# Two-layer feed-forward after retention: shifted loads in the first layer only, four groups, two banks begun with partial sums, another order of conversions, second pass backwards

## The chip, the core and the metric

The kernel runs on one core of one Trainium2 chip. The metric is the time of one execution on the device in microseconds (us). The number to predict is a median of runs of the changed kernel.

TensorE is called PE here (PEld are its weight loads), VectorE is DVE, ScalarE is ACT, GpSimd is POOL, and SP is the engine whose queue issues every DMA of this kernel.

## The reference

```python
# retention: B=2, H=8, S=768, D=64
for t in range(S):
    state = gamma * state + k[t] outer v[t]
    y[t] = scale * q[t] @ state
x = y as (1536 tokens, 512)
h = x @ moe_w_in                      # 512 -> 2048
x = softplus(h) @ moe_w_out           # 2048 -> 512   (layer 1)
h = x @ moe2_w_in
out = silu(h) @ moe2_w_out            #               (layer 2)
```

The four weight matrices are 64-bit floats in memory.

## The kernel before

Every matrix product is made of three matmuls: a float is kept as a high part (rounded to the fast format fp32r) and a low part (the rest), and low·high, high·low and high·high are added up in PSUM.

**Conversion of weights.** A weight tile of 128 x 512 64-bit numbers (512 KB) is brought in by `w_load` into one of three buffers (`rc`, "raw"). ACT takes the exponent (`w_exponent`, L357). DVE takes the digits (`w_digits`) and forms the low part (`w_values`, L378 to L386). ACT forms the high part (`w_split`, L399). For tiles from number `NEAR` on, a second load of the same tile, displaced by two bytes (`near_load`, L339), lets one shift (L364) give the digits, which otherwise takes two operations (L369, L370).

**Layer 1** runs in 48 steps. The 16 blocks of 128 inner columns (`fc`) are cut into groups (`GROUPS`), and within a group the three token blocks of 512 follow one another. A step does `first(i)` (12 matmuls into bank `h`, L447, then softplus on ACT) and `second(i - 2)` (12 matmuls into four banks `acc0` to `acc3`, L486). At the end of a group and block, `evacuate` adds the four banks to `part` on DVE (L497; the first group copies instead). PE's order is thus first, second, first, second. Conversions of later tiles are laid into the steps by `_jobs`, which goes through the steps, gains `STEP_ROOM` in each and spends `TILE_COST` or `FORMS_COST`. A job has three parts: a start (exponent), a main part in the same step, and an end in the next step.

**Layer 2** uses a seven-product scheme (products P1 to P7 of quarter matrices). Its weights need, beside conversion, sums of quarters: `w_sums` and `w_keep`, together called "forms". The two `w_in` tiles of a pair (s = 0) are converted into the buffer `st1`; forms turns `st1` into seven quarters with low parts, and one DMA stores them to DRAM (`d1`, L420, 1792 KB). The `w_out` tiles (s = 1) are converted into `st2` and stored to `d2` (L403, 512 KB). `w32` is scratch for the sums. Later `q1_load` (L563) and `q2_load` (L567) bring the stored forms back. There are 8 pairs of blocks and 2 passes over the tokens, so 16 pair steps, q0 to q15. What layer 1's steps had no room for is left for the first pair steps, in "slots" after some of the products: a slot ends the job before, and does the main part of the next one.

In a pair step, products P1, P6, P2, P7, P5, P4, P3 (L580) alternate with "fill": the second matmuls (L612) of the pair before. Between products ACT and DVE work on the banks: ACT copies P1's bank into P6's (L652), and keeps the others (L655, L661); DVE makes c22 after P5 (L664) and c12 after P3 (L670); ACT does silu twice (L594, L595) and DVE the low part (L596). P3 adds into the bank that L664 has read, so it waits for L664. Every engine and SP's queue work strictly in program order.

## Time and profile before

| | |
|---|---|
| median of 3 runs | 607.4 us (606.79 to 607.94) |
| the profiled execution: its own time | 611.62 us |
| the profiled execution: span of its instructions | 609.2 us |
| PE busy, of the span | 567.9 us (93%) |
| DVE busy | 366.1 us (60%) |
| ACT busy | 245.2 us (40%) |
| mean granted TensorE clock | 0.974 of full speed |

The busy shares are means over stages of different kinds: retention (to about 66 us), layer 1 (to about 306 us), layer 2 with conversions still running (to about 440 us), and layer 2 alone. All times inside the program below are us from the start of the span.

### The profile page before, as it was taken

How to read it: one execution, taken by the hardware profiler on the slowest of the kernel's cores; microseconds unless marked ns; L12 is line 12 of the kernel's file. 1: busy time of each engine (PE TensorE's matmuls, PEld its weight loads, DVE VectorE, ACT ScalarE, POOL GpSimd, SP SyncE). 2: the span in 40 equal slices, each digit the busy share in tenths (PEclk: the TensorE clock that was granted, in tenths of full speed). 3: DMA queues.
4: the chain of work that ended last, by engine and by line, in shares of the span. 5: the costliest groups of instructions: out<-in, count | busy, mean ns of one | idle time of the engine just before them, and what ended most of it. 6: DMA issues, size and time to landing. Idle time of an engine off the chain costs nothing.

```text
span 609.2 us, 8166 instructions
## 1 busy us (share of the span) xinstructions
PE 567.9 (93%) x3122; PEld 485.7 (80%) x3122; DVE 366.1 (60%) x642; ACT 245.2 (40%) x461; POOL 25.6 (4%) x24
## 2 busy tenths in 40 slices
PE   7899999999999999999997689496899999999997
PEld 5777888888888888888886578386788999999996
DVE  3877847987888789768846757566464222122212
ACT  2354535544344433435443535244354433333332
POOL 1554000000000000000000000000000000000000
PEclk9999999999999999999998989697899999999999
DMA  8993323886848777777459999898374754445412
GB/s 304 357 386 115 105 103 105 305 280 210 294 152 297 248 247 292 275 267 280 167 202 357 384 333 411 299 409 323 153 280 180 277 207 190 190 189 190 190 69 103
DMA packets 32453, 148.10 MB, mean 243 GB/s; under 512 B 3616, under 2 KB 3616, under 8 KB 28064
## 3 DMA queue, kind: packets, MB, share of 16 engines
q1 hardware_dynamic: 32416, 147.60, 66.1%
q8 instruction: 24, 0.39, 0.3%
q14 instruction: 13, 0.11, 0.0%
HBM read 121.37 MB, written 26.21 MB: 242 GB/s over the span
## 4 chain that ended last, share of the span: by engine, by line
PE 75%; DMA 12%; DVE 8%; ACT 2%; issue 2%; SPq 0%; DVEq 0%; ACTq 0%
PE acc L486 21%; PE h L447 21%; PE acc L612 15%; DMA d<-st 7%; PE by L580 6%; PE bz L580 4%; PE bx L580 4%; DMA rr<-in_att 3%; DMA rc<-in_wts 1%; PE sc L231 1%; DMA rp<-in_att 1%; PE py L249 1%; DVE w L407 1%; DVE rc L381 1%; PE py L271 1%
## 5 line engine op out<-in xcount | busy, mean ns | idle before, releaser
L447 PE MATMUL h<-rx,rw 128*128 128x512 f32 (+1 forms) x588 | 139.4, 386 | 0.1
L486 PE MATMUL acc<-rg,rw 128*128 128x512 f32 x564 | 136.5, 390 | 0.0
L612 PE MATMUL acc<-rw,rg 128*128 128x512 f32 x477 | 130.6, 405 | 0.0
L447 PEld LDWEIGHTS h<-rx,rw 128*128 128x128 f32 x588 | 108.6, 188 | 22.4 <-DVE rx L294 0.3
L486 PEld LDWEIGHTS acc<-rg,rw 128*128 128x128 f32 x564 | 105.7, 188 | 21.8 <-issue 0.4
L612 PEld LDWEIGHTS acc<-rw,rg 128*128 128x128 f32 x477 | 92.2, 196 | 12.9
L466 ACT ACTIVATE rg<-h 128x512 fp32r<-128x512 f32 x47 | 28.0, 597 | 115.5 <-PE h L447 115.5
L596 DVE TENSOR_TENSOR rg<-re,rg 128x384 fp32r<-128x384 f32 x53 | 29.3, 557 | 72.3 <-ACT re L595 72.3
L386 DVE SCALAR_TENSOR_TENSOR st<-rc 128x512 fp32r<-128x512 int32 x32 | 22.2, 692 | 44.5 <-DMA d<-st 43.7
L381 DVE SCALAR_TENSOR_TENSOR rc<-rc 128x512 uint32<-128x512 uint32 x64 | 44.3, 692 | 2.2
L357 ACT ACTIVATE rc<-rc 128x512 f32<-128x512 f32 x64 | 41.8, 668 | 5.4 <-DMA rc<-in_wts 3.9
L399 ACT ACTIVATE st<-rc 128x512 fp32r<-128x512 f32 x32 | 20.0, 632 | 49.3 <-DMA d<-st 43.2
L580 PE MATMUL bz<-f,rw 128*128 128x384 f32 x96 | 22.3, 373 | 17.9 <-DVE rp L664 17.9
L378 DVE TENSOR_SCALAR rc<-rc 128x512 uint32<-128x512 uint32 x64 | 27.0, 422 | 19.5 <-ACT rc L357 19.5
L594 ACT ACTIVATE rg<-rp 128x384 fp32r<-128x384 f32 x32 | 16.7, 522 | 49.0 <-DVE rp L670 24.8
L580 PEld LDWEIGHTS bz<-f,rw 128*128 128x128 f32 x96 | 18.8, 208 | 20.6 <-DVE rp L664 19.6
L473 DVE TENSOR_TENSOR rg<-re,rg 128x512 fp32r<-128x512 f32 x47 | 34.0, 723 | 1.1 <-ACT re L467 1.0
L497 DVE TENSOR_TENSOR rp<-acc,rp 128x512 f32<-128x512 f32 x48 | 31.0, 684 | 4.2 <-PE acc L486 4.2
L580 PE MATMUL by<-rx,rw 128*128 128x384 f32 x144 | 29.8, 342 | 2.9 <-ACT rp L655 2.9
L580 PEld LDWEIGHTS by<-rx,rw 128*128 128x128 f32 x144 | 26.4, 193 | 5.8 <-ACT rp L655 3.4
L580 PE MATMUL by<-f,rw 128*128 128x384 f32 x144 | 29.3, 338 | 0.0
L384 DVE TENSOR_SCALAR rc<-rc 128x512 uint32<-128x512 uint32 x64 | 27.3, 427 | 2.2
(82 smaller groups left out, 630.1 us busy)
## 6 DMA issues: line engine op xcount, KB each, us to landing
rc<-in_wts SPq DMA_DIRECT2D x64, 512.0 KB, 5.0
rw<-d SPq DMA_DIRECT2D x16, 1792.0 KB, 7.9
near<-in_wts SPq DMA_DIRECT2D x53, 511.5 KB, 4.6
rw<-d SPq DMA_DIRECT2D x16, 1024.0 KB, 9.7
d<-st SPq DMA_DIRECT2D x8, 1792.0 KB, 7.0
d<-st SPq DMA_DIRECT2D x16, 512.0 KB, 5.4
rp<-in_att SPq DMA_DIRECT2D x8, 512.0 KB, 7.0
out<-rp SPq DMA_DIRECT2D x12, 256.0 KB, 2.0
```

The source lines that it names most:

```text
L357: nc.scalar.activation(out=z, in_=raw_t[u][:, :, 1].bitcast(F32), func=AF.Copy, scale=2.0**-112)
L378: nc.vector.tensor_scalar(out=z, in0=z, scalar1=3, scalar2=4, op0=ALU.logical_shift_left, op1=ALU.bitwise_or)
L381: nc.vector.scalar_tensor_tensor(out=a, in0=raw[:, :, 1], scalar=0x80000000, in1=z, op0=ALU.bitwise_and, op1=ALU.bitwise_or)
L384: nc.vector.tensor_scalar(out=z, in0=a, scalar1=0xFF800000, scalar2=None, op0=ALU.bitwise_and)
L447: nc.tensor.matmul(ph[:, t], lhsT=w[:, s], rhs=x[:, kc, t], start=kc == o == j == 0, stop=kc == NPAIR - 1 and j == 2, skip_group_check=i == 0,
L466: nc.scalar.activation(out=ghi, in_=ph, func=AF.Softplus)
L473: nc.vector.tensor_tensor(out=glo, in0=t, in1=ghi.bitcast(F32), op=ALU.subtract)
L486: nc.tensor.matmul(acc_t[m], lhsT=lhsT, rhs=rhs, start=(first and j == 0), stop=(last and j == 2))
L497: nc.vector.tensor_tensor(out=to, in0=acc_t[m], in1=to, op=ALU.add)
L580: nc.tensor.matmul(to, lhsT=a[:, s], rhs=x[:, kc, :], start=start and kc == j == 0, stop=kc == 1 and j == 2, skip_group_check=True,)
L596: nc.vector.tensor_tensor(out=glo, in0=r, in1=ghi.bitcast(F32), op=ALU.subtract)
L612: nc.tensor.matmul(acc2_t[m], lhsT=a[:, s], rhs=b, start=start and j == 0, stop=stop and j == 2)
```

## The change

- `GROUPS` becomes (3, 4, 4, 5): four groups instead of five, so 12 evacuations of four banks instead of 15.
- Banks 0 and 1 (`SEEDED`) are no longer added to `part` by DVE. When a group ends, ACT copies the bank out to `part`, then copies the sum so far of the next group and block into the bank, and that block's matmuls all accumulate on it. Banks 2 and 3 are added by DVE as before.
- Of a layer 2 pair, the order is now: both s = 0 tiles, forms, both s = 1 tiles. The s = 1 tile of an odd block goes to `w32` instead of `st2`. The end of forms is divided: ACT's copy (`w_sums_high`) comes at the start of the next slot, DVE's subtraction and the store (`w_keep`) at its end.
- The displaced loads stop with the last tile of layer 1's steps. The tiles left for layer 2's slots use the two-operation digits.
- `_jobs` has other numbers: 20 tiles and 5 forms of layer 2 are done in layer 1's steps instead of 16 and 3, and 12 tiles and 3 forms are left instead of 16 and 5. A pair step has three slots (P1, P6, P5) instead of four.
- The second pass takes the pairs from 7 to 0, so two of `q1_load` and two of `q2_load` fall away at the turn. `q1_load(0)` is issued after step 45 instead of 41, and the preparation of layer 2's left operands is one step earlier.

```diff
-GROUPS = (3, 3, 3, 3, 4)
+GROUPS = (3, 4, 4, 5)
+SEEDED = (0, 1)
...
-STEP_ROOM = 5.0
+STEP_ROOM = 5.3
...
-        second += [("tile", 1, 2 * p + j, s) for j in range(2) for s in range(2)] + [("forms", 1, p, 0)]
+        a, b = 2 * p, 2 * p + 1
+        second += [("tile", 1, a, 0), ("tile", 1, b, 0), ("forms", 1, p, 0), ("tile", 1, a, 1), ("tile", 1, b, 1)]
...
+        k = (0, 1, 2, 1, 0, 2)[u] if u < 6 else (1, 0, 2)[u % NRAW]
...
     def near_load(u):
-        if u >= len(tiles):
+        if u >= NEAR[1]:
...
-            hi, lo = st2[:, 0:512], st2[:, 512:1024]
+            t = (st2, w32)[fc % 2]
+            hi, lo = t[:, 0:512], t[:, 512:1024]
...
+    def w_sums_high():
         nc.scalar.activation(out=st1[:, 1024:2048].bitcast(F32R), in_=st1[:, 3072:4096], func=AF.Copy)
...
-                    acc_t[m], lhsT=lhsT, rhs=rhs, start=(first and j == 0), stop=(last and j == 2)
+                    start=first and j == 0 and not seeded,
...
-            if g > 0:
+            if m in SEEDED:
+                nc.scalar.activation(out=to, in_=acc_t[m], func=AF.Copy)
+                if i + 1 < N and steps[i + 1][0] > 0:
+                    acc_t[m] = psa.tile([P, BLK], F32, tag=f"acc{m}", name=f"acc{i + 1}_{m}")
+                    b1 = steps[i + 1][1]
+                    nc.scalar.activation(out=acc_t[m], in_=part[:, m, b1 * BLK : (b1 + 1) * BLK], func=AF.Copy)
+            elif g > 0:
                 nc.vector.tensor_tensor(out=to, in0=acc_t[m], in1=to, op=ALU.add)
...
+    def pair_of(q):
+        return q if q < NPR else 2 * NPR - 1 - q
...
-        if q < NQ:
-            nc.sync.dma_start(out=q1[q % 2], in_=d1[q % NPR])
+        if q < NQ and not NPR <= q < NPR + 2:
+            nc.sync.dma_start(out=q1[pair_of(q) % 2], in_=d1[pair_of(q)])
...
+    def job_last(j):
+        if j[0] == "forms":
             w_keep(j[2])
...
-            if i == 41:
+            if i == 45:
                 q1_load(0)
...
-                work = {"P1": (slot,), "P6": (slot,), "P7": (slot,), "P5": (slot,)}
+                work = {"P1": (slot,), "P6": (slot,), "P5": (slot,)}
```

How the rows stand on the engines, at three places. First DVE, in a pair step of layer 2 before: from one forms to the next writing of `st_883` (that is `st1`; `w_884` is `w32`, `st_885` is `st2`).

```order
L413 TENSOR_TENSOR st_883<-w_884,st_883 128x256
L596 TENSOR_TENSOR rg<-re,rg 128x384 x2
L670 TENSOR_TENSOR rp<-bz_2751,rp 128x384
L596 TENSOR_TENSOR rg<-re,rg 128x384
L417 TENSOR_TENSOR st_883<-st_883 128x1024
L364 TENSOR_SCALAR rc<-near 128x512
L378 TENSOR_SCALAR rc<-rc 128x512
L381 SCALAR_TENSOR_TENSOR rc<-rc 128x512
L384 TENSOR_SCALAR rc<-rc 128x512
L386 SCALAR_TENSOR_TENSOR st_883<-rc 128x512
```

The same place in the changed kernel: its first lines are the end of a tile into `st2` and `w_keep` (now L425), the last line is the next writing of `st_883` (now L392).

```order
L392 SCALAR_TENSOR_TENSOR st_885<-rc 128x512
L425 TENSOR_TENSOR st_883<-st_883 128x1024
...
L392 SCALAR_TENSOR_TENSOR w_884<-rc 128x512
L621 TENSOR_TENSOR rg<-re,rg 128x384
L689 TENSOR_TENSOR rp<-bz_3045,rp 128x384
L375 TENSOR_SCALAR rc<-rc 128x512
L376 SCALAR_TENSOR_TENSOR rc<-rc 128x512
L384 TENSOR_SCALAR rc<-rc 128x512
L387 SCALAR_TENSOR_TENSOR rc<-rc 128x512
L390 TENSOR_SCALAR rc<-rc 128x512
L392 SCALAR_TENSOR_TENSOR st_883<-rc 128x512
```

Between `w_keep`, whose store reads `st1`, and the next writing of `st1` there stood only the four operations of one conversion; now a whole tile into `w32`, a low part and the c22 sum stand between as well, and the digits are two rows (L375, L376).

Second ACT, at the end of a group in layer 1 of the changed kernel (L474 and L475 are softplus of a step, L405 the end of the conversion before, L363 an exponent).

```order
L474 ACTIVATE rg<-h_1182 128x512
L475 ACTIVATE re<-h_1182 128x512
L405 ACTIVATE rw<-rc 128x512
L405 ACTIVATE st_883<-rc 128x512
L363 ACTIVATE rc<-rc 128x512
L512 ACTIVATE rp<-acc_0_1031 128x512
L516 ACTIVATE acc_0_1207<-rp 128x512
L512 ACTIVATE rp<-acc_1_1034 128x512
L516 ACTIVATE acc_1_1210<-rp 128x512
L474 ACTIVATE rg<-h_1228 128x512
```

Before, DVE had four rows L497 at such a place and ACT none; now ACT has the four rows L512 and L516, and DVE the sums of banks 2 and 3.

Third SP's queue, around the first loads of forms, before (`d_0_78` is `d1[0]`, `d_3_89` is `d2[3]`):

```order
L563 DMA rw<-d_0_78 128x3584
L403 DMA d_3_89<-st_885 128x1024
L339 DMA near<-in_wts 128x2046
L330 DMA rc<-in_wts 128x1024
L339 DMA near<-in_wts 128x2046
L330 DMA rc<-in_wts 128x1024
L403 DMA d_3_89<-st_885 128x1024
L563 DMA rw<-d_1_79 128x3584
```

and in the changed kernel:

```order
L335 DMA rc<-in_wts 128x1024 x3
L428 DMA d_4_82<-st_883 256x1x1792
L409 DMA d_4_90<-st_885 128x1024
L409 DMA d_4_90<-w_884 128x1024
L588 DMA rw<-d_0_78 128x3584
L588 DMA rw<-d_1_79 128x3584
L592 DMA rw<-d_0_86 128x2048
L335 DMA rc<-in_wts 128x1024
L588 DMA rw<-d_2_80 128x3584
```

The load of `d1[0]` now stands directly ahead of that of `d1[1]`, behind all stores of layer 1's steps, and no displaced load follows.

## Rows read from the trace of the kernel before

**Rows 1.** The page: PE's busy tenths in 40 slices of the span.

```profile
PE   7899999999999999999997689496899999999997
```

**Rows 2.** Windows: layer 1, pair step q0, q0 to q5, and q7.

```profile
core 0: us, PE busy (x) PEld busy (x) DVE busy (x) ACT busy (x) POOL busy (x), PEclk, DMA share, GB/s
66.00:306.00 240.00, 240.00 (x1059) 198.62 (x1058) 190.86 (x341) 106.80 (x191) 0.00 (x0) 1.00 0.66 228
306.04:321.08 15.04, 13.13 (x68) 11.73 (x66) 6.86 (x12) 6.86 (x13) 0.00 (x0) 1.00 0.64 220
306.04:440.04 134.00, 103.83 (x458) 90.19 (x457) 80.16 (x151) 52.69 (x102) 0.00 (x0) 0.89 0.85 321
456.25:471.91 15.66, 15.66 (x79) 14.10 (x78) 7.10 (x11) 6.50 (x13) 0.00 (x0) 1.00 0.49 185
```

**Rows 3.** Waits from 300 to 450: engine, line, waited for, us, times, longest.

```profile
DVE st L386 <- DMA d<-st: 34.0, 6, 8.5
```

**Rows 4.** Timeline of DVE, then PE, around one stall: start, us, work, [idle before, releaser].

```profile
376.38 1.23 DVE L417 TENSOR_TENSOR st<-st 128x1024 fp32r<-128x1024 f32 x1 [1.13 <-ACT st L414]
...
387.98 0.69 DVE L386 SCALAR_TENSOR_TENSOR st<-rc 128x512 fp32r<-128x512 int32 x1 [8.52 <-DMA d<-st]
...
392.25 2.29 PE L580 MATMUL bz<-f,rw 128*128 128x384 f32 x6 [8.13 <-DVE rp L664]
```

**Rows 5.** Timeline of PE in q8 and q9 without waits: P5, P3, then P1, P6.

```profile
481.59 1.22 PE L580 MATMUL bz<-f,rw 128*128 128x384 f32 x6
...
485.78 1.22 PE L580 MATMUL bz<-rx,rw 128*128 128x384 f32 x6
...
487.54 1.22 PE L580 MATMUL bx<-f,rw 128*128 128x384 f32 x6
...
489.98 1.22 PE L580 MATMUL by<-f,rw 128*128 128x384 f32 x6
```

**Rows 6.** Groups by line and form: count, busy us, mean ns, idle before.

```profile
L381 DVE SCALAR_TENSOR_TENSOR rc<-rc 128x512 uint32<-128x512 uint32 x64 | 44.3, 692 | 2.2
L364 DVE TENSOR_SCALAR rc<-near 128x512 uint32<-128x512 uint32 x53 | 22.3, 421 | 0.4
L370 DVE SCALAR_TENSOR_TENSOR rc<-rc 128x512 uint32<-128x512 uint32 x11 | 8.3, 758 | 0.4
L407 DVE TENSOR_TENSOR w<-st 128x1024 f32<-128x1024 f32 x8 | 9.7, 1218 | 0.0
L411 DVE TENSOR_TENSOR st<-st,w 128x256 f32<-128x256 f32 x8 | 3.4, 425 | 0.3
L596 DVE TENSOR_TENSOR rg<-re,rg 128x384 fp32r<-128x384 f32 x53 | 29.3, 557 | 72.3 <-ACT re L595 72.3
L497 DVE TENSOR_TENSOR rp<-acc,rp 128x512 f32<-128x512 f32 x48 | 31.0, 684 | 4.2 <-PE acc L486 4.2
L594 ACT ACTIVATE rg<-rp 128x384 fp32r<-128x384 f32 x32 | 16.7, 522 | 49.0 <-DVE rp L670 24.8 <-DVE rp L664 24.2
L652 ACT ACTIVATE by<-bx 128x384 f32<-128x384 f32 x16 | 7.6, 474 | 4.4 <-PE bx L580 4.4
L499 ACT ACTIVATE rp<-acc 128x512 f32<-128x512 f32 x6 | 3.4, 598 | 0.6 <-PE acc L486 0.6
L357 ACT ACTIVATE rc<-rc 128x512 f32<-128x512 f32 x64 | 41.8, 668 | 5.4 <-DMA rc<-in_wts 3.9 <-DVE st L386 1.1
```

**Rows 7.** One line's DMAs: L420 (stores of `d1`), then L563 (loads of it).

```profile
DMA to landing us min/median/max: 6.1/7.0/10.3
DMA to landing us min/median/max: 7.1/7.9/9.8
```

**Rows 8.** Timeline of PE after waits of two lengths.

```profile
321.08 1.76 PE L580 MATMUL bx<-rx,rw 128*128 128x384 f32 x6 [1.91 <-ACT re L595]
322.63 2.72 PE L612 MATMUL acc<-rw,rg 128*128 128x512 f32 x6
...
337.19 1.33 PE L580 MATMUL bz<-rx,rw 128*128 128x384 f32 x6 [1.34 <-ACT re L595]
```

More of the change, by code (lines that the diff above doesn't have):

```diff
@@ L65, in _steps @@
     return steps
-STEP_ROOM = 5.0
+STEP_ROOM = 5.3
 TILE_COST = 2.75
 FORMS_COST = 4.1
-LATE = (44, 45, 46, 47)
+LATE = (43, 44, 45, 46, 47)
 def _jobs(steps):
@@ L92, in _jobs @@
         if steps[i][4]:
-            room -= 2.75 if steps[i][0] else 1.4
+            room -= 1.4
         ready = [u for u in left if last.get((u[0] - NSLOT, u[1]), -1) < at]
@@ L105, in _jobs @@
             while n < 2 and room >= (cost := FORMS_COST if second[0][0] == "forms" else TILE_COST):
+                if second[0][0] == "forms" and jobs[-1][1] == 1 and jobs[-1][4] == at:
+                    break
                 jobs.append((*second.pop(0), at))
@@ L321, in retention_ffn2_kernel @@
     order = {j[:4]: u for u, j in enumerate(tiles)}
-    NEAR = next(u for u, j in enumerate(tiles) if j[4] == 10)
+    NEAR = next(u for u, j in enumerate(tiles) if j[4] == 10), next(u for u, j in enumerate(tiles) if j[4] is None)
     def w_load(u):
@@ L328, in w_load @@
         _, l, fc, s, _ = tiles[u]
-        t = rc[:, u % NRAW * 1024 : (u % NRAW + 1) * 1024].bitcast(U32)
+        k = (0, 1, 2, 1, 0, 2)[u] if u < 6 else (1, 0, 2)[u % NRAW]
+        t = rc[:, k * 1024 : (k + 1) * 1024].bitcast(U32)
         nc.sync.dma_start(out=t, in_=wts[l, fc, s].bitcast(U32))
@@ L362, in w_digits @@
         conv_t[u] += (m,)
-        if u >= NEAR:
+        if NEAR[0] <= u < NEAR[1]:
             nc.vector.tensor_scalar(
@@ L402, in w_split @@
             o = fc % 2 * 1024
-            nc.sync.dma_start(out=d2[fc // 2][:, o : o + 1024], in_=st2)
+            nc.sync.dma_start(out=d2[fc // 2][:, o : o + 1024], in_=(st2, w32)[fc % 2])
     def w_sums():
@@ L480, in gemm2 @@
         for m in ms:
-            if first:
+            seeded = g > 0 and m in SEEDED
+            if first and not seeded:
                 acc_t[m] = psa.tile([P, BLK], F32, tag=f"acc{m}", name=f"acc{i}_{m}")
@@ L486, in gemm2 @@
                 nc.tensor.matmul(
-                    acc_t[m], lhsT=lhsT, rhs=rhs, start=(first and j == 0), stop=(last and j == 2)
+                    acc_t[m],
+                    lhsT=lhsT,
+                    rhs=rhs,
+                    start=first and j == 0 and not seeded,
+                    stop=last and j == 2,
+                    skip_group_check=m in SEEDED,
                 )
@@ L559, in retention_ffn2_kernel @@
     NQ = NPASS * NPR
+    def pair_of(q):
+        return q if q < NPR else 2 * NPR - 1 - q
     def q1_load(q):
-        if q < NQ:
-            nc.sync.dma_start(out=q1[q % 2], in_=d1[q % NPR])
+        if q < NQ and not NPR <= q < NPR + 2:
+            nc.sync.dma_start(out=q1[pair_of(q) % 2], in_=d1[pair_of(q)])
     def q2_load(q):
-        if q < NQ:
-            nc.sync.dma_start(out=q2[q % 2], in_=d2[q % NPR])
+        if q < NQ and not NPR <= q < NPR + 2:
+            nc.sync.dma_start(out=q2[pair_of(q) % 2], in_=d2[pair_of(q)])
     gc_t, acc2_t = {}, {}
@@ L573, in product @@
         wo = QF * WFORMS.index(wf)
-        w = q1[q % 2].bitcast(F32R)
+        w = q1[pair_of(q) % 2].bitcast(F32R)
         whi, wlo = w[:, wo : wo + QF], w[:, 7 * QF + wo : 8 * QF + wo]
@@ L607, in unit @@
             acc2_t[m] = pool.tile([P, DM], F32, tag=tag, bufs=1, name=f"acc_{q}_{m}")
-        w = q2[q % 2].bitcast(F32R)
+        w = q2[pair_of(q) % 2].bitcast(F32R)
         whi, wlo = w[:, 1024 * fc : 1024 * fc + 512], w[:, 1024 * fc + 512 : 1024 * fc + 1024]
@@ L702, in job_end @@
         else:
+            w_sums_high()
+    def job_last(j):
+        if j[0] == "forms":
             w_keep(j[2])
@@ L709, in step @@
         first(i)
-        for j in split_units:
+        ended = split_units
+        for j in ended:
             job_end(j)
@@ L717, in step @@
             job_main(j)
+        for j in ended:
+            job_last(j)
         act2(i)
@@ L861, in retention_ffn2_kernel @@
         near_ring = _Ring(pool.tile([P, 2048], F32, name="near"), 0, 1024, 2)
-        near_load(NEAR)
-        near_load(NEAR + 1)
+        near_load(NEAR[0])
+        near_load(NEAR[0] + 1)
         x0 = x_make(0)
-        more = {42: x0[0][:2], 43: x0[0][2:], 45: x0[1], 46: x0[2], 47: x0[3]}
+        more = {41: x0[0][:2], 42: x0[0][2:], 44: x0[1], 45: x0[2], 46: x0[3]}
         for i in range(NLEAD + 2, N):
             step(i, more.get(i, ()))
-            if i == 41:
+            if i == 45:
                 q1_load(0)
@@ L878, in slot @@
         def slot():
-            for j in before:
+            ended = before.copy()
+            for j in ended:
                 job_end(j)
@@ L890, in slot @@
                 before.append(j)
+            for j in ended:
+                job_last(j)
         x1 = []
```

## The prediction

> **What bounds the kernel now.** I began with the page's busy tenths [rows 1]. PE reads 9 almost everywhere; the exceptions are the first slice (loads of the inputs) and slices 21 to 29. Means would hide this: DVE's 60% and ACT's 40% are of no use until one knows which of them PE waits for in those slices. So next I read the stages by windows [rows 2]. In layer 1 PE is busy for 240.00 of 240.00 us: nothing that DVE, ACT or the queues gain there can shorten it. The 1059 matmuls in it give 0.227 us each, so a step of 24 takes 5.44 us and each half of it 2.72. Pair step q7, with no conversions, is 15.66 us, again all PE. But q0 to q5, where the left conversions run in the slots, take 134.00 us with 103.83 busy. Without waits they would take 13.13 (q0's own PE time, it has less fill) + 5 x 15.66 = 91.4. So **42.6 us** are lost there, to waits and to the lower clock after them (0.89 granted). That is the whole stock from which this change can take.
>
> The chain behind these waits is in two views. In the list of waits, DVE stood 34.0 us in 6 waits for the stores from the stage buffers [rows 3]. The timeline shows one of them link by link [rows 4]: `w_keep` starts at 376.38 and its store reads `st1`; the next tile's low part goes into `st1` and waits 8.52 us; DVE works in order, so the c22 sum (L664) queued behind it is late; P3 adds into the bank that L664 reads, and PE stands for 8.13 us. The resource is not DVE's time but one buffer, rewritten immediately behind its own store.
>
> **The change, part by part.** *Order of conversions.* After `w_keep` there now come two s = 1 tiles, into `st2` and `w32`, before `st1` is written again. For F5 (the forms of pair 5; the digit is the pair) the store is issued in q1's P6 slot and `st1` is rewritten in q2's P1 slot, five products and their fill later, about 13 us by the 15.66 of a pair step. The store lands in 6.1 to 10.3 us [rows 7]: no wait. For F6 the store leaves in q3's P1 slot, about 6 us into the step, and the rewriting is due in its P5 slot after about 8 us more: a wait of 0 at the median 7.0, up to 2 at 10.3. I take 0.4. After F7 nothing more goes into `st1`. So the 42.6 us lose their cause, and what is left is DVE's own work.
>
> *Two-operation digits.* A tile with the displaced load costs DVE two operations of 0.692 (L381's kind) and three of 0.421 (L364's kind), 2.65 us; the new digits add L370's 0.758 [rows 6], so 3.41. Twelve tiles: +9.1 us of DVE in the slots. In exchange twelve loads of 512 KB leave queues that were 0.85 busy there [rows 2]; nobody on the path waited for them, so that is worth 0 by itself.
>
> *What PE still waits for.* Forms costs DVE 1.218 + 4 x 0.425 = 2.92, then `w_keep` 1.23 [rows 4, 6]. Three slots hold at most about 3.41 + 3.41 + 2.92 + 1.23 = 11.0, and DVE's own work in a pair step is six operations of 0.557, 3.3: 14.3 of 15.66 us. It fits, but in order, so I follow the tightest place. From P5's end to P3's end PE takes 485.78 - 481.59 = 4.19 us [rows 5]. DVE in that time has c22 (0.56), the P5 slot's tile (3.41) and two low parts (1.11), 5.08, so the c12 sum starts 0.89 late. Behind it stand c12 0.56, two silus of 0.52 and the copy into P6's bank 0.47 [rows 6], 2.07 in all, against 2.98 us from P3's end to the next P6 (1.76 - 1.22 + 2.44, rows 5's starts). The slack is 0.91, so a plain tile costs PE nothing. Where it is exceeded: q0 has one fill unit less after P5 (0.70) and an evacuation (0.68, L497) in DVE's way: 5.08 + 0.68 - 3.49 - 0.91 = 1.3. In q1 forms, `w_keep` and two tiles meet. DVE comes out of q0 about 6 us late (a tile, a low part, an evacuation and the 1.3), so the sums end 9 us into q1; ACT's `w_sums_high` (about 1) and an exponent (0.67) stand before the first silu, which frees P2's bank at 11.6, where P5 wants it at 10.8: 0.85. The c12 sum is then 1.6 late, less the slack: 0.65. Together 1.5. q2 has forms in P5, less than a tile: 0. q3: the 0.4 above. q4 has a tile and `w_keep` in P5: 5.08 + 1.23 - 4.19 - 0.91 = 1.2. Sum **4.4 us**, with 0 and about 8 as bounds (all stores at 7.0 and DVE always early; all at 10.3).
>
> *Fewer groups, seeded banks, more conversions in layer 1.* DVE loses 48 sums of 0.684 and keeps 18, and loses three copies: -22.6. It gains four tiles and two forms: 4 x 2.65 + 2 x 4.15 = +18.9. So it stays near 187 of 240 us. ACT gains 18 copies out, 18 seeds and three copies of the first group, at 0.598 each (L499) [rows 6] 23.3 us, and some 7 for the added conversions: 137 of 240. No row shows a copy from SBUF into PSUM; from below L652's 0.474 (PSUM to PSUM, 384 columns), from above L357's 0.668; I take L499's. None of this is on PE's path as long as a seed is there in time: the four ACT copies take 2.4 us, and from bank 1's last matmul to its next use PE has 1.36 + 2.72 = 4.1 us of other matmuls. Queued behind the seeds on ACT is the next softplus, which PE wants a step later. I take 0. Two places are tight: in steps 27 and 39 `st1` is rewritten one step after `w_keep`, so DVE waits 2 to 3 us for the store. PE needs a low part only two steps (10.9 us) after its softplus, which covers that. Bound 0 to 8.5 us (rival B).
>
> *`q1_load(0)` later.* It now waits for the last use of its buffer in step 45, and P1 follows four halves later: 10.9 us against 7.1 to 9.8 for landing [rows 7]: 0. *Second pass backwards:* four loads less where PE is full anyway [rows 2]: 0. The other buffer numbers in `w_load` move two early loads; PE does not wait for those: 0.
>
> Sum: -42.6 + 4.4 = -38.2. The profiled execution took 611.62, so 573.4 by its own clock; set against the median of 607.4 it is **569.2 us**.
>
> **Rivals.** *A, the slots stay slow* (0.20). The stores land at 10.3 instead of 7.0 (+3.3) and each of four remaining waits is followed by matmuls at half rate. After a wait of 1.91 us, P1 took 1.76 instead of 1.22 and six fill matmuls took 2.72 instead of 6 x 0.227 [rows 8], 1.9 us more. After 1.34 us there was no such loss (1.33). For: DVE has 1.4 us to spare in a pair step. Against: the waits worked out are all at or under 1.5. Time 569.2 + 3.3 + 4 x 1.9 = 580.1. [...]
>
> *B, layer 1 is no longer all PE* (0.12). The seeds come 0.5 us late at each of nine group ends and the two rewritings of `st1` cost 2 us each: 8.5, so 577.7. For: ten tiles fall in steps 35 to 42, two per step in four of them, 5.3 us of DVE in 5.44. Against: 53 us of DVE's 240 are free.
>
> *C, slower than before* (0.02). A seed stands on ACT behind the exponents (L357), which wait for raw loads; PE would wait at each of nine group ends. It decides from 38.2 / 9 = 4.2 us each; at a whole step, 9 x 5.44 = 49, 618.2. Against: all 64 exponents together waited 3.9 us for loads [rows 6].
>
> *D, the wait only moves* (0.03): the stores hold up `st1` after F5 and F6, or `w32`, as before, 34.0 / 6 = 5.7 us each, and the half rate follows: 569.2 + 2 x (5.7 + 1.9) = 584.4.
>
> **How the numbers follow.** The forecast has 0.63, with a range of its own from 564.8 (all 42.6 come back) to 574. The whole range is 564.8 to 580, which takes in A and B nearly whole and leaves out C, D and the far ends. A measurement of this kernel tells 0.2% (1.2 us) from no change. Only C is slower, 0.02; 0.01 for no change out of D; faster 0.97.
>
> **What would show it.** Right: PE full from 66 to about 306 as before; q0 to q5 in about 96 us; waits of DVE for the stage stores nearly gone after 306, at most one in q3; the slots' digits as pairs of 0.42 and 0.76; PE's remaining waits behind the c12 chain, each under 2 us; q6 beginning near 402. Wrong: PE idle before 306 with ACT's copies or DVE as the releaser (B, C); waits for stores of over 5 us (D); granted clock well under 1.0 in q1 to q4 (A). The forecast is too high if the slots run without any wait, too low if DVE's order costs more than I followed.

## The result and the profile after

The changed kernel takes 583.58 us (median of 4 runs, 582.17 to 584.82) against 607.67 for the kernel before on the same chip: ratio **0.9603** [0.9574, 0.9633]. It is faster by 24.1 us; 569.2 was forecast, a gain of 38.2, and the time lies 3.6 us above the range. The profiled execution took 582.73 us, its span 580.6. Line numbers grow by some 25 in layer 2: L580 is now L605, L652 is L677, L664 is L689, L670 is L695; in layer 1, L486 is L495, L386 is L392, L407 is L413, L414 is L422.

The page's busy tenths of PE and its granted clock, which answer to [rows 1]:

```profile
PE   8999999999989989999999999899999999999997
PEclk9999999999999997999999999899999999999999
```

The hole of slices 21 to 29 is gone, but there are small dents now in slices 12, 15 and 26, with a lower clock in 16 and 26, and the first two lie in layer 1, where before there was none. Windows of layer 1, q0, q0 to q5, q3 and q7, which answer to [rows 2]:

```profile
core 0: us, PE busy (x) PEld busy (x) DVE busy (x) ACT busy (x) POOL busy (x), PEclk, DMA share, GB/s
66.00:312.45 246.45, 241.41 (x1047) 197.84 (x1046) 188.79 (x340) 131.25 (x234) 0.00 (x0) 0.99 0.70 252
312.45:325.42 12.97, 12.97 (x67) 11.90 (x66) 4.35 (x9) 8.09 (x15) 0.00 (x0) 1.00 0.63 226
312.45:412.01 99.56, 94.21 (x458) 83.40 (x457) 68.56 (x127) 47.68 (x94) 0.00 (x0) 0.98 0.82 306
359.31:379.79 20.48, 17.49 (x79) 15.43 (x78) 17.11 (x32) 8.83 (x17) 0.00 (x0) 0.92 0.91 332
427.67:443.33 15.66, 15.66 (x80) 14.09 (x79) 7.11 (x11) 6.50 (x13) 0.00 (x0) 1.00 0.18 67
```

q0 to q5 went from 134.00 to 99.56 us, near the forecast of about 96. Layer 1 grew: from the first matmul into an `acc` bank to q0's P1 it took 242.4 us before and 251.7 now. In q0 to q5 DVE no longer waits for a store out of `st1` or `st2`, where [rows 3] had 34.0 us. New in the list of waits are these (columns as in [rows 3]; 66 to 412):

```profile
DVE w L413 <- DMA d<-w: 6.7, 2, 4.0
DVE rc L370 <- DMA near<-in_wts: 8.5, 4, 2.6
PE acc L495 <- ACT acc L516: 4.4, 3, 3.1
PE by L605 <- ACT by L677: 4.8, 4, 3.0
```

L413 is the first sum of forms. It writes the scratch `w32`, which since this change also holds each odd s = 1 tile while that tile is stored. Both waits for it reach PE. The first, in layer 1 (timeline of all engines; start, us, work, idle before and its releaser):

```profile
202.10 1.00 SPq L409 DMA_DIRECT2D d<-w  x1
...
212.75 1.23 DVE L413 TENSOR_TENSOR w<-st 128x1024 f32<-128x1024 f32 x1 [2.67 <-DMA d<-w]
...
215.60 1.06 ACT L422 ACTIVATE st<-st 128x1024 fp32r<-128x1024 f32 x1 [4.08 <-DVE st L419]
216.56 1.21 ACT L363 ACTIVATE rc<-rc 128x512 f32<-128x512 f32 x2
...
218.29 0.60 ACT L516 ACTIVATE acc<-rp 128x512 f32<-128x512 f32 x1
...
218.94 5.49 PE L495 MATMUL acc<-rg,rw 128*128 128x512 f32 x12 [3.10 <-ACT acc L516]
```

The store issued at 202.10 lands at 212.6. DVE's sums for F2 (forms of pair 2) are late; ACT's copy of the sums (L422, `w_sums_high`) stands in ACT's order ahead of the exponents and the seeds; PE waits 3.10 us for a seed and then runs 12 matmuls in 5.49 us instead of 2.88 (granted clock 0.50 from 218.9 to 224.5). The second, in the slots:

```profile
342.46 1.18 SPq L588 DMA_DIRECT2D rw<-d  x1
...
343.73 1.38 SPq L592 DMA_DIRECT2D rw<-d  x1
...
346.50 0.32 SPq L409 DMA_DIRECT2D d<-w  x1
...
359.29 1.22 DVE L413 TENSOR_TENSOR w<-st 128x1024 f32<-128x1024 f32 x1 [4.02 <-DMA d<-w]
...
364.91 2.18 PE L605 MATMUL by<-rx,rw 128*128 128x384 f32 x6 [2.99 <-ACT by L677]
```

Here the store stands behind 2816 KB of pair loads and takes 12.7 us. The sums for F6 are late by 4.02, DVE's c12 behind them too, then ACT's copy into P6's bank, then PE: 2.99 us, and 2.18 for six matmuls that otherwise take 1.21 (granted clock 0.54 from 364.9 to 367.0; [rows 8] showed 1.76 for six after a wait of 1.91). Landings, first of L409 (stores of s = 1 tiles, 512 KB), then of L428 and L588, which answer to [rows 7]:

```profile
DMA to landing us min/median/max: 4.6/8.7/14.7
```

```profile
DMA to landing us min/median/max: 6.2/6.9/8.6
```

```profile
DMA to landing us min/median/max: 7.0/7.8/12.0
```

The medians of the large stores and loads are as before. On the page, where the stores of s = 1 tiles had a median of 5.4 us before, they now have (KB each, median us to landing):

```profile
d<-st SPq DMA_DIRECT2D x8, 512.0 KB, 8.6
d<-w SPq DMA_DIRECT2D x8, 512.0 KB, 9.2
```

Groups by form, of [rows 6]: the seed (L516), the copy out (L512), and the added digit operation (L376):

```profile
L512 ACT ACTIVATE rp<-acc 128x512 f32<-128x512 f32 x24 | 13.9, 587 | 0.2 <-PE acc L495 0.2
L516 ACT ACTIVATE acc<-rp 128x512 f32<-128x512 f32 x18 | 10.8, 602 | 0.6
L376 DVE SCALAR_TENSOR_TENSOR rc<-rc 128x512 uint32<-128x512 uint32 x23 | 15.9, 693 | 0.8
```

### The profile page after: what moved, and what is told of

Read it like the earlier page. It is cut to its first block, busy times and chain, and to the rows that moved or that the text cites. A ratio compares the mean times of both kernels' runs of the same rounds, so it can differ in the third digit from the quotient of the medians.

```text
span 580.6 us, 8107 instructions
## 1 busy us (share of the span) xinstructions
PE 562.8 (97%) x3122; PEld 479.9 (83%) x3122; DVE 353.7 (61%) x621; ACT 267.3 (46%) x500; POOL 25.6 (4%) x24
## 4 chain that ended last, share of the span: by engine, by line
PE 71%; DVE 13%; DMA 9%; ACT 4%; issue 1%; SPq 1%; POOL 0%; DVEq 0%; POOLq 0%
PE acc L637 19%; PE acc L495 17%; PE h L455 15%; PE by L605 8%; PE bx L605 5%; PE bz L605 5%; DMA d<-w 4%; DMA near<-in_wts 2%; DVE rc L387 2%; DMA d<-st 1%; DMA rp<-in_att 1%; PE sc L235 1%; PE py L253 1%; DVE rc L384 1%; DVE rc L390 1%
## 5 line engine op out<-in xcount | busy, mean ns | idle before, releaser
L495 PE MATMUL acc<-rg,rw 128*128 128x512 f32 x564 | 140.0, 396 | 5.0 <-ACT acc L516 4.4
L495 PEld LDWEIGHTS acc<-rg,rw 128*128 128x128 f32 x564 | 106.8, 191 | 29.2 <-ACT acc L516 5.9
L637 PE MATMUL acc<-rw,rg 128*128 128x512 f32 x477 | 125.4, 392 | 0.0
L637 PEld LDWEIGHTS acc<-rw,rg 128*128 128x128 f32 x477 | 88.7, 188 | 12.3
L474 ACT ACTIVATE rg<-h 128x512 fp32r<-128x512 f32 x47 | 28.0, 596 | 92.2 <-PE h L455 92.1
L363 ACT ACTIVATE rc<-rc 128x512 f32<-128x512 f32 x64 | 41.5, 665 | 5.7 <-DMA rc<-in_wts 5.4
L605 PE MATMUL by<-rx,rw 128*128 128x384 f32 x144 | 30.4, 347 | 4.8 <-ACT by L677 4.8
L605 PEld LDWEIGHTS by<-rx,rw 128*128 128x128 f32 x144 | 26.2, 192 | 8.2 <-ACT by L677 6.5
L689 DVE TENSOR_TENSOR rp<-bz,rp 128x384 f32<-128x384 f32 x16 | 8.9, 557 | 38.8 <-PE bz L605 38.8
L605 PE MATMUL by<-f,rw 128*128 128x384 f32 x144 | 29.2, 337 | 0.0
L475 ACT ACTIVATE re<-h 128x512 f32<-128x512 f32 x48 | 28.5, 593 | 0.0
L605 PEld LDWEIGHTS by<-f,rw 128*128 128x128 f32 x144 | 25.9, 188 | 2.0
L405 ACT ACTIVATE rw<-rc 128x512 fp32r<-128x512 f32 x32 | 20.2, 633 | 15.7 <-DVE rc L387 15.7
L637 PE MATMUL acc<-rw,rx 128*128 128x512 f32 x99 | 27.1, 399 | 0.0
```

What stands on the lines that cost most here:

```text
L363: nc.scalar.activation(out=z, in_=raw_t[u][:, :, 1].bitcast(F32), func=AF.Copy, scale=2.0**-112)
L474: nc.scalar.activation(out=ghi, in_=ph, func=AF.Softplus)
L475: nc.scalar.activation(out=t, in_=ph, func=AF.Softplus)
L495: nc.tensor.matmul(acc_t[m], lhsT=lhsT, rhs=rhs, start=first and j == 0 and not seeded, stop=last and j == 2, skip_group_check=m in SEEDED,)
L605: nc.tensor.matmul(to, lhsT=a[:, s], rhs=x[:, kc, :], start=start and kc == j == 0, stop=kc == 1 and j == 2, skip_group_check=True,)
L637: nc.tensor.matmul(acc2_t[m], lhsT=a[:, s], rhs=b, start=start and j == 0, stop=stop and j == 2)
```

## The experiments

All runs in one table. "Layer 1" is the time from the first `acc` matmul to q0's P1, "q0 to q5" that from there to q6's P1, both from PE's timeline. Ratios are to the kernel before on the same chip. One per cent is 6.1 us.

| run | median us | ratio, interval | layer 1 | q0 to q5 |
|---|---|---|---|---|
| before, first / second trace | 607.67 | 1 | 242.4 / 242.4 | 134.0 / 132.7 |
| changed kernel | 583.58 | 0.9603 [0.9574, 0.9633] | 251.7 | 99.6 |
| own_buf | 576.24 | 0.9457 [0.9430, 0.9483] | 247.0 | 98.4 |
| high_late | 581.82 | 0.9556 [0.9521, 0.9590] | 249.8 | 100.7 |
| no_seeds | 585.39 | 0.9605 [0.9572, 0.9639] | 253.0 | 98.0 |
| own_spread | 574.32 | 0.9415 [0.9379, 0.9450] | 244.7 | 98.6 |
| loads_late | 578.91 | 0.9490 [0.9457, 0.9523] | 244.7 | 100.2 |
| mid_loads | 573.83 | 0.9436 [0.9407, 0.9465] | 245.8 | 96.5 |
| before_order | 602.74 | 0.9883 [0.9850, 0.9916] | 242.2 | 128.0 |
| order_near1 | 594.29 | 0.9774 [0.9742, 0.9806] | 242.2 | 118.9 |
| old_order | 632.87 | 1.0369 [1.0333, 1.0404] | 278.6 | 122.8 |
| near_all | 583.17 | 0.9579 [0.9550, 0.9609] | 252.7 | 99.3 |
| four_slots | 591.63 | 0.9720 [0.9699, 0.9740] | 251.5 | 108.9 |
| forward | 583.79 | 0.9590 [0.9562, 0.9618] | 252.3 | 99.4 |
| mix | 584.87 | 0.9616 [0.9594, 0.9637] | 244.9 | 107.4 |
| mix2 | 586.67 | 0.9635 [0.9611, 0.9659] | 245.5 | 108.0 |
| near_p6 | 585.91 | 0.9621 [0.9594, 0.9648] | 244.1 | 107.9 |
| near_p1 | 574.61 | 0.9432 [0.9406, 0.9457] | 245.1 | 99.3 |

**Where the miss lies: the scratch buffer.** Theory W: the second use of `w32` costs both large waits. Rivals: the seeds, or ACT's order. `own_buf` takes the second use away: odd s = 1 tiles go to `f0` (idle in layer 1 until step 42) or, in the slots, into the buffer of the displaced loads, which is idle there.

```diff
+    def odd_home(at):
+        if at is None:
+            return nt[:, 0:1024]
+        return f0[:, 0:1024] if at < 42 else w32
-            t = (st2, w32)[fc % 2]
+            t = odd_home(at) if fc % 2 else st2
```

> The changed kernel, but the odd s = 1 tiles get buffers of their own (the free f0 in layer 1, the displaced loads' buffer in the slots) instead of the scratch w32 that forms writes too. Theory W (the shortfall is two waits of forms for w32, which is still being stored: F2 in layer 1 and F6 in q3, both under landings of 10.5 and 12.7 us): DVE's waits for the stores from w32 vanish, so do the PE waits of 3.1 at the seeds of step 30 and of 3.0 in q3 with their half-clock stretches (3.3 and 1.8 us), and the time falls by about 11 us, to 572 to 574. Rival L (layer 1 and the slots are simply overfull, DVE and the queues are late whatever waits): the waits reappear at other places, the time falls by under 3 us, to 581 or more.

Both waits for L413 are gone, and Rival L is out. 576.24 is, by its ratio, 0.0146 x 607.67 = 8.9 us under the changed kernel, where theory W expected about 11. The stages of the traced execution show 5.8 of that (it took 578.16): 4.6 in layer 1, at the first wait's place, and 1.2 in q0 to q5. There q3 fell to 15.66, but q4 rose to 19.4: freed of one wait, DVE met the store of F6 out of `st1`, in the slots (timeline; L433 is the forms' store, L397 the low part):

```profile
361.98 0.53 SPq L433 DMA_DIRECT2D d<-st  x1
...
372.49 0.69 DVE L397 SCALAR_TENSOR_TENSOR st<-rc 128x512 fp32r<-128x512 int32 x1 [2.43 <-DMA d<-st]
...
375.99 1.58 PE L610 MATMUL by<-rx,rw 128*128 128x384 f32 x6 [1.86 <-ACT by L682]
```

PE's wait of 1.86 us was followed by a granted clock of 0.61 (375.95 to 380.00). So the store of F6, too, would have been late; in the changed kernel the wait for `w32` ahead of it hid that.

`high_late` keeps `w32` and moves ACT's copy behind the seeds, in layer 1 alone:

```diff
         second(i - LAG)
+        for j in ended:
+            if j[0] == "forms":
+                job_end(j)
         for j in split_units:
             job_main(j)
```

> The changed kernel, but in layer 1's steps ACT's copy at the end of forms stands behind the evacuation and the seeds instead of ahead of them. Theory W with the order on ACT as its second link: forms in step 29 are as late as before, but the seeds of step 30 no longer stand behind them; layer 1 gets back the wait of 3.1 and its half-clock stretch, about 6 us, 577 to 578; q3 keeps its 3.0. Rival L: DVE's lateness reaches PE in another way (low parts, sums of banks 2 and 3), under 2 us.

It brought about half of what was expected or less, 0.0047 x 607.67 = 2.9 us by the ratios, whose intervals overlap, and 1.9 in layer 1 of the trace, where 6 were forecast: PE no longer waited for that seed, but 2.50 us for a low part of softplus, since DVE itself was late by the wait for `w32`. `no_seeds` sets `SEEDED = ()`, so that DVE adds all four banks as before:

> The changed kernel with no seeded banks: all four banks are added by DVE at a group's end, as before the change (36 sums of 0.68 instead of 18, 12.3 us more of DVE; 18 copies out and 18 seeds less on ACT). If the seeds are what layer 1 loses by, rather than DVE's lateness, PE's waits of 4.4 us for the seeds and the half clock after them go and the time falls by 5 to 7, to 577. Theory W expects the lateness of DVE at step 29 to hit the four sums instead (they stand in DVE's order right behind the waiting forms): PE waits for the banks there too, and since DVE has 12 us more to do the time is the same or some us more, 583 to 588.

The same time as the changed kernel. Layer 1 waits again, now for DVE (2.82, 1.55, 1.28 and 0.50 us) and once for ACT's softplus (1.16), so the seeds do not cause the loss. That they bring no gain is shown only with the wait for `w32` in place; no run leaves them out of `own_buf`. A second trace of the kernel before, for the size of what differs between executions:

> The kernel before, a second trace. The first one's own time (611.6) was 4 us above the median of its runs. If that execution was long by its start, layer 1 begins near 60.8 here, as in the changed kernel, instead of 63.6, and q0 to q5 are again near 134 us; if it was long by the slots, q0 to q5 take nearer 130.

Layer 1 and q0 to q5 repeat within 1.3 us; the start, before layer 1's first `acc` matmul, took 62.4 instead of 63.6.

**The rest of layer 1.** `own_spread` is `own_buf` with `LATE = (18, 20, 43, 44, 45, 46, 47)`, so that steps 18, 20 and 21, which each held two tiles, hold one.

> Here the odd s = 1 tiles have a stage of their own, as in the run before with that edit (576.2), and steps 18 and 20 take no second-layer job, so that the second tiles of steps 18, 20 and 21 move to 19, 21 and 23; from step 24 on nothing changes. Theory (the waits of 0.85, 1.00 and 0.19 us at 166 to 173 come from near loads that land in 7 to 8 us where two tiles stand in one step): they go, layer 1 falls from 247.0 to between 244 and 245.5, and the time to between 573 and 575. Rival (DVE is simply overloaded in that stretch, loads or not): the waits stay or move to step 23, and the time is the same within 1 us.

The waits at 166 to 173 went, layer 1 is 244.7, within 2.3 us of before. (The traced execution took 581.51, 7 us over the median; 6.7 more than in the changed kernel lie ahead of the first `acc` matmul.) 0.9415 against 0.9457 is 2.6 us; the intervals overlap a little, so the time alone would not show it, but the stage does.

**Which part makes the slots fast.** The prediction gave the whole gain to the order of conversions. `before_order` is the kernel before with the new order and the second use of `w32`, nothing else (21 jobs are left for the slots as before, now 17 tiles and 4 forms). Of its edit, the order:

```diff
-        second += [("tile", 1, 2 * p + j, s) for j in range(2) for s in range(2)] + [("forms", 1, p, 0)]
+        a, b = 2 * p, 2 * p + 1
+        second += [("tile", 1, a, 0), ("tile", 1, b, 0), ("forms", 1, p, 0), ("tile", 1, a, 1), ("tile", 1, b, 1)]
```

> The kernel before with the new order of the second-layer conversions and the second home of the odd s = 1 tiles alone; groups, displaced loads everywhere, jobs of layer 1 and direction of the second pass stay as they were. Theory (the order alone takes the stores' waits out of q0 to q5): q0 to q5 fall from 133 to between 97 and 103, layer 1 grows by 2 to 8 us through the second use of the scratch buffer, the time is between 575 and 583. Rival (the gain needs the four jobs fewer in the slots and the loads taken out of them): q0 to q5 stay over 112, time over 590.

The theory fell: 128.0 us, 5 to 6 less than before; by the ratio the whole gain is 0.0117 x 607.67 = 7.1 us. Layer 1 did not grow (242.2): there forms stand at least three steps behind the odd tile whose store they wait for, in the changed kernel F2 stands two behind it. The list of waits in q0 to q5, and the window:

```profile
DVE rc L366 <- DMA near<-in_wts: 20.4, 6, 10.0
...
DVE w L409 <- DMA d<-w: 8.9, 2, 6.2
```

```profile
303.91:431.94 128.03, 101.41 (x457) 87.58 (x456) 78.90 (x149) 52.81 (x103) 0.00 (x0) 0.89 0.92 348
```

The 34.0 us for the stores are gone as forecast, and DVE now waits for displaced loads and for `w32` instead; the queues are busy 0.92 of the time. The longer wait for `w32` goes straight to PE, in q2 (DVE, then PE):

```profile
358.29 1.23 DVE L409 TENSOR_TENSOR w<-st 128x1024 f32<-128x1024 f32 x1 [6.20 <-DMA d<-w]
...
361.62 2.29 PE L582 MATMUL bz<-f,rw 128*128 128x384 f32 x6 [7.20 <-DVE rp L666]
```

These 7.20 are a good quarter of the 26.5 us for which PE waits in q0 to q5 there. So the new home holds this run back too, and what the order alone is worth with a buffer of its own was not measured. The other way round, `old_order` is the changed kernel with the old order. It keeps the second home, so that forms now stand right behind the odd tile that is being stored out of `w32`:

> The changed kernel with the old order of the second-layer conversions (both tiles of a left block, both of the right, then the forms); everything else of the change stays. Theory (it is the order that pays): st1 is again rewritten right behind its own store, q0 to q5 go back to between 115 and 134, the time is between 595 and 612. Rival (fewer jobs in the slots and fewer loads there pay): q0 to q5 stay under 108 and the time under 592.

Slower than before, and by its ratio (1.0369 - 0.9603) x 607.67 = 47 us slower than the changed kernel. Waits from 200 to 330 there:

```profile
ACT st L405 <- DMA d<-st: 33.1, 3, 13.3
DVE rc L384 <- ACT rc L363: 33.0, 9, 9.4
...
PE acc L495 <- DVE rg L481: 16.0, 4, 8.1
...
DVE w L413 <- DMA d<-w: 10.5, 3, 4.2
...
PE acc L495 <- ACT acc L516: 8.7, 1, 8.7
```

In layer 1, with six jobs more, the old order costs 27 us: ACT's high part waits for the store out of `st1`, the exponents stand behind it, DVE behind those, and DVE waits 10.5 us for `w32` besides. In q0 to q5 it costs 23 us, and there the list has for `w32`:

```profile
DVE w L413 <- DMA d<-w: 22.8, 3, 9.3
```

So the 47 us belong to the old order and the second home together. 7 and 47 are not the worth of one edit in two kernels: the kernel before has no store out of `w32` at all, and here DVE's waits for that store are as long as the loss in the slots. What else the slots need was asked part by part. `order_near1` is `before_order` without displaced loads in the slots; `near_all` is the changed kernel with them:

```diff
-        if u >= NEAR[1]:
+        if u >= len(tiles):
...
-        if NEAR[0] <= u < NEAR[1]:
+        if NEAR[0] <= u:
```

> The kernel before with the new order and the second home, and with displaced loads in the first part only (none for tiles converted in the slots); groups and jobs of layer 1 as before, so 21 jobs in the slots where the changed kernel has 15. Theory (order and loads are two limits one behind the other, and both have to go): q0 to q5 fall from 128.0 with the order alone to between 100 and 112, time between 576 and 588. Rival (the jobs have to go too: 21 jobs make DVE or the queues the bound): q0 to q5 stay over 118, time over 593.

> The changed kernel with the displaced loads kept in the slots too, as before: digits in one operation, twelve loads of 512 KB more. Theory (in the slots the transfers bound as much as the stores: with the order alone q0 to q5 kept 128 us, with DVE 20.4 us at displaced loads): q0 to q5 rise from 99.6 to between 108 and 120, time between 592 and 604. Rival (it is the six jobs fewer in the slots, four tiles and two forms, that pay; the loads were worth nothing, as the prediction had it): q0 to q5 within 97 to 103, time within 4 us of the changed kernel.

With 21 jobs in the slots the displaced loads cost 9 us (6.6 by the ratios), and 118.9 is left, as the rival had it. With 15 jobs they cost nothing on balance (99.3 against 99.6): q3 is 2.6 us longer, where the store out of `w32` lands in 14.2 us instead of 12.7, and q1, q2 and q5 are 2.9 shorter, where a tile costs DVE 2.65 us instead of 3.41. This is so although the queues were as busy as in `before_order` (window of `near_all`, q0 to q5):

```profile
314.75:414.00 99.25, 94.50 (x457) 84.15 (x456) 60.41 (x115) 47.52 (x94) 0.00 (x0) 0.97 0.92 359
```

So the theory written for `near_all` fell, and what pays is fewer jobs, and fewer of them in a pair step. `four_slots` has the 15 jobs of the changed kernel, but a slot behind P7 as before, up to four jobs in a pair step:

> The changed kernel with a slot behind P7 again in each pair step, so that the 15 jobs left stand up to four in a pair step, as the 21 did before. Theory (it is the density, four jobs in 15.66 us of PE, that made DVE and the loads late; a job is about 2.65 to 4.15 us of DVE beside 3.3 us of its own): q0 to q5 rise from 99.6 to between 108 and 122, time 591 to 606. Rival (the number of jobs in all sets the loss, and a wait costs the same wherever the jobs stand): q0 to q5 stay within 96 to 103, time within 4 us of the changed kernel.

108.9: 9.4 us of the gain are the density alone. Two lines of it, DVE and PE in the slots:

```profile
381.80 1.22 DVE L413 TENSOR_TENSOR w<-st 128x1024 f32<-128x1024 f32 x1 [7.30 <-DMA d<-w]
...
385.14 2.29 PE L605 MATMUL bz<-f,rw 128*128 128x384 f32 x6 [6.28 <-DVE rp L689]
```

Packed closer, the store out of `w32` has still less time. From 118.9 to 108.9, at four slots and with no displaced loads in either, go with the six jobs that left (the other parts of the change differ too between those two).

**Second pass.** `forward` takes the pairs in the old direction in both passes:

> The changed kernel with the second pass forwards, so that four loads of pair factors (two of 1792 KB, two of 1024 KB) come back around q8. Prediction's term 0: PE is full there, time the same within 1 us, q6 to q15 at 15.65 each. Rival: the loads at the turn are late and PE waits in q8 or q9 by over 1 us each.

The same; q6 to q14 are 15.62 to 15.66 us each.

**Can loads and stores both be in time?** A pair's first factors are what `q1_load` brings (1792 KB), its second factors what `q2_load` brings (1024 KB). These runs are `own_spread` with the pair loads elsewhere in SP's order (`near_p6`, `near_p1` and `mix` also with displaced loads in the slots and the odd tile in `w32` there). The edit, for `loads_late`; `mid_loads` has the first `if` alone and leaves `q1_load` where it was:

```diff
+            if name == "P1" and q > 0:
+                q2_load(q)
+            if name == "P6" and q > 0:
+                q1_load(q + 1)
...
-        q2_load(q + 1)
```

> The last edit with the pair loads of the slots issued elsewhere in SP's order: the second factors of a pair when its step begins, the first factors of the next pair behind product P6 instead of one pair step earlier, so that no stage store is queued behind both. Theory (the wait that is left in q4, 1.86 us, is a store for which DVE waits because it shares the queues with 2.8 MB of pair loads): the store lands in about 7 us instead of 10.4, q4 falls from 19.4 to between 16 and 17.5, the time by 2 to 3 us. Rival (the store is slow in any case, or the pair loads come too late for P1 now): q4 keeps its wait, or another pair step shows PE waiting for a load of 1 us or more, and the time is the same or longer.

F6's store was in time (8.0 us), but the first factors were late: PE stood 2.93 us for them in q3.

> Own stage and spread steps, and of the pair loads only the second factors later (when their pair step begins); the first factors leave where they did in the changed kernel. Theory (one of the two loads fewer ahead of the forms' store lets it land in time, and the wait of 2.93 us for a load that the run with both loads later showed is gone): the store of F6 lands in 7 to 9 us, q4 falls from 19.5 to between 15.7 and 17.5, time 2 to 4 us under the run with own stage and spread steps (574.3, at 609.97 before). Rival (1792 KB of first factors alone hold the store up): q4 stays over 19.

q4's wait was 1.47 us and the granted clock was 1.00 in q0 to q5 (96.5), but the edit is not the cause, since it moved nothing. The pair loads ahead of F6's store leave at the same place, 0.19 us into q3 for the second factors; first `mid_loads`, then `own_spread`:

```profile
352.98 0.33 SPq L593 DMA_DIRECT2D rw<-d  x1
353.66 0.33 SPq L597 DMA_DIRECT2D rw<-d  x1
```

```profile
358.52 0.33 SPq L593 DMA_DIRECT2D rw<-d  x1
359.20 0.33 SPq L597 DMA_DIRECT2D rw<-d  x1
```

In both kernels the second factors' load waits for PE to be done with its buffer. F6's store took 10.0 us against 10.6, not 7 to 9, and the time is that of `own_spread`. So this run is in effect a repeat, which shows that the wait in q4 (1.47, 1.86 in `own_buf`, 2.03 in `own_spread`) and the slow stretch behind it differ between executions.

> Displaced loads in the slots too, odd s = 1 tiles in a stage of their own in layer 1 and in the scratch buffer in the slots, steps 18 and 20 without second-layer jobs, and the second factors loaded behind product P7 of their own pair step, so that they stand behind the store out of the scratch buffer. With displaced loads everywhere q0, q1, q2, q4 and q5 took 12.98, 16.07, 15.65, 15.67 and 15.82 us and only q3 waited (4.73). Theory (that store lands in time when 1024 KB fewer stand ahead of it): q3 falls to between 15.7 and 18, q0 to q5 to between 92 and 95, time between 567 and 572. Rival (the queues are full with twelve loads more; the store is late in any case): q3 keeps over 4 us of wait or another store or load takes its place, time over 573.

> As the run with the second factors loaded when their pair step begins (573.8, q0 to q5 96.5), but loaded behind product P7 of it, so that fewer bytes stand ahead of the forms' store in q3. Theory: q4's last wait of 1.47 us shrinks or goes, q0 to q5 between 94.5 and 96.5, time the same or up to 2 us less. Rival: the second factors now come late for the fill of the next pair step, and PE waits for a load by over 1 us: 575 or more.

> As the run with displaced loads in the slots and the second factors behind P7 (its only waits over 0.3 us in q0 to q6 were 5.87, 4.87 and 0.81 us for those second factors), but the second factors loaded two products earlier, behind P6 and its stores. Theory (what is left is the load's place alone): the waits for the second factors shrink to under 2 us each or go, q0 to q5 between 92 and 96, time 567 to 573. Rival (they still come late, or the store out of the scratch buffer does): one wait of over 3 us stays, time over 575.

> The same with the second factors loaded when their pair step begins, ahead of the store out of the scratch buffer. Theory: no wait for the second factors; the store out of the scratch buffer decides q3: it stood 4.73 us of PE with 2816 KB ahead of it, and here 1024 KB of these leave at nearly the same time, so 0 to 5 us in q3; q0 to q5 between 92 and 98, time 567 to 575. Rival: another store or load takes its place, time over 576.

With the second factors behind P7 or P6, PE waits for these. One of the waits in `mix`, fill matmuls in q2:

```profile
341.83 2.93 PE L640 MATMUL acc<-rw,rg 128*128 128x512 f32 x6 [5.87 <-DMA rw<-d]
```

In `mix` and `near_p6` nothing else in q0 to q5 waited for over 0.3 us; in `near_p1` the loads were in time and the store out of `w32` was not (one wait of 4.78). There, too, the second factors leave within 0.5 us of where they did in `near_all`, and q3 is the same (23.1). Each order that did move a load (`loads_late`, `mix`, `mix2`, `near_p6`) moved the wait to another transfer. `own_spread`, `mid_loads` and `near_p1` are the fastest found, alike within their intervals and some 10 us under the changed kernel.

## Why the prediction was wrong

It missed by 583.58 - 569.2 = 14.4 us. By stages, in the traces, forecast against measured:

- *Layer 1 and the seeds, "I take 0"*: +9.3. This is the largest failing term. The two rewritings of `st1` in steps 27 and 39 were as written (DVE waited 1.73 and 3.12 us for the store, PE at most 0.42). What was put at nothing is `w32`: the section on the order of conversions put the odd tile "into `st2` and `w32`" and asked only when `st1` is written again. `w32` was scratch of the next forms, so the wait removed at `st1` came back at `w32`; `own_buf`, without it, has 4.6 us less. Another 2.4 went when steps with two tiles were spread (`own_spread`), with the waits of 0.22, 1.11 and 0.19 us there. The last 2.3 stay open; `own_spread` shows 1.4 us of waits in layer 1.
- *Slots, "4.4 us of waits"*: +3.8. q0 came out 1.5 and q4 1.2 under the forecast, q1, q2 and q5 0.4, 0.7 and 0.9 over it, and q3 4.4 over: `w32` again, with the half clock behind it. The step that failed is "q2 has forms in P5, less than a tile: 0": those forms had to wait 4.02 us for a store issued in q2's P1 slot, and PE paid in q3. A store of 512 KB was never given a time; before, their median on the page was 5.4 us, and now 8.6 (`st2`) and 9.2 (`w32`), 12.7 at the one that counts. That the sum came within 3.8 is in part luck: the waits forecast for q0 and q4 did not come, and others came in their place.
- *Start and q6*: -3.4. Before the first `acc` matmul it took 60.8 instead of 63.6 us; that differs between executions (62.4 in the second trace of before). q6 took 15.66 instead of 16.22 (16.12 in the second trace). With some -0.3 elsewhere, these make the 9.3 us between -38.2 and what the profiled executions show, 611.62 - 582.73 = 28.9.
- *The baseline*: the other 5.1. The profiled execution of before lay 4.2 us over the median shown, and terms read from it were taken from the median; that of after lay 0.85 under its median. The second trace of before took 609.04: 1.2 us less at the start and 1.3 in q0 to q5.

**The mechanism was wrong as well**, though the forecast for the slots came out near. "So the 42.6 us lose their cause, and what is left is DVE's own work" was said of the order. The order with the second home leaves 128.0 us. Three things stood behind the stores out of `st1`, and all were to be read before. First, the store out of `w32`, as above. Second, [rows 2] has the queues 0.85 busy over 134.00 us, 113.9 us of transfers; at 0.93, the most that any of these runs kept over q0 to q5 (`near_p1`), they would need about 122 us by this estimate, whatever the order. The forecast counted twelve loads as leaving, not the two forms' stores and four tiles with their loads and stores; after, it is 0.82 x 99.56 = 81.6 us. Third, taking the displaced loads out relieves the queues but fills DVE: four tiles of 3.41 us and its own 3.3 make 16.9 us in a pair step of 15.66, where tiles of 2.65 make 13.9. The text worked out that three slots fit and never that four don't, so it could not see what three slots were worth (`order_near1`, `four_slots`).

That these three are what held `before_order` and `order_near1` is argued from waits, shares and sums; the runs show only which parts give the time back. The third is too small by itself: it gives 1.3 us a pair step, while q1 to q5 of `order_near1` are 2.2 to 8.9 over 15.66, DVE is busy for 90.3 of 118.9 us there, and DVE's longest waits for a transfer are for `w32` (8.0 us in two waits). How the rest divides between them stays open.

What was right: the stores out of `st1` and `st2` no longer stop DVE in q0 to q5 of the changed kernel, though for F6 only because DVE was late already (2.43 us in `own_buf`, where the text took 0.4); 0 for the second pass (`forward`); seeds of about 0.598 (0.602 measured). "So that is worth 0 by itself" of the displaced loads fits `near_all`, but as a balance of 2.6 us against 2.9, and with 21 jobs they were worth 9. That seeds hold up PE (rival B) came true in three waits of 4.4 us in all, the one of 3.10 through ACT's order and not by the seeds' own length. Rival D named `w32` with 0.03 but priced it for the slots alone; that its 584.4 lies near the measured time is luck, since only 3.8 us of the miss lie in the slots. Rival A's half clock was seen only behind the two waits of about 3 us; the other waits of the changed kernel, up to 1.11, were followed by none. [rows 8] set 1.91 against 1.34 as if the length decided; in the same trace a wait of 2.92 us (at 333.14) was followed by six matmuls in 1.33, with no loss.

## What to carry to other kernels

When a wait is taken away by giving a buffer to a second user, look up the buffer's first user and price that wait with landing times from a stretch in which the queues are as full, not with a median over all stretches (here 12.7 us where the page's median was 5.4). Before a stall's whole length is booked as a gain, work out what the same stretch needs of every other resource (share times length for the queues, jobs times duration for an engine): here the order with the second home gave 7 us where the stalls were 34. Look in the trace whether an edit changed what it was to change: `mid_loads` wrote a load elsewhere in the program, and it left at the same moment. Take terms from one execution only against that execution's time, and expect the difference to the median to come back.

## What was not expected of the hardware

- The landing of one 512 KB store ranged from 2.6 to 10.7 us in the kernel before and from 3.9 to 16.0 in `before_order` (median 10.0). The one of 12.7 us in the changed kernel was issued behind 2816 KB of loads; The store of F6 (1792 KB) took 10.4 us in `own_buf`, issued 6 us behind both loads of a pair, and 8.0 in `loads_late`, behind one.
- 16 DMA engines at a share of 0.92 moved 359 GB/s in `near_all`, for 99 us, without PE waiting for a load (it waited 4.73 us behind a store).
- The length of PE's wait alone did not tell whether half rate followed. It did after 1.86 us in `own_buf`, 1.91 in the kernel before and 2.50 in `high_late`; it did not after 1.84 (`four_slots`), 2.48 (`no_seeds`), 2.92 (the kernel before) and 2.93 (`loads_late`). After a wait of 2.03 us in `own_spread` the first product ran at full rate (1.33 us) and the slow ones came 1 to 3 us later (1.93 instead of 1.21, granted clock 0.55 from 382.50 to 384.50).
